# A fused attention, channel-mix and mixture-of-experts kernel: expert remainders of at most 32 rows move from full 128-row slots to small float32 slots on four quarters of TensorE's columns

## The chip, the cores and the metric

One core of one Trainium2 chip. The metric is the device time of one execution in microseconds (us), the median of several. A difference of about 0.2% is what a measurement of this kernel can tell from none.

## The reference, cut to what matters

Block-causal attention (4 batches, 8 heads, 576 tokens, head width 64) feeds a channel mix (512 to 1024 to 512, in float64 weights), and its output `x` feeds a mixture of 8 experts in which each token goes to one expert:

```python
fresh_e = argmax(logits[b, s]); e = fresh_e if s == 0 or local_gate[b, s] < 0.5 else prev_e
h = np.maximum(x[b, s] @ w1[e], 0.0)          # 512 -> 1024
out[b, s] = p[e] * (h @ w2[e])                # 1024 -> 512
```

There are 2304 tokens. On the inputs used, the reference sends 0, 1196, 0, 1, 361, 285, 457 and 4 tokens to experts 0 to 7.

## The kernel before

The kernel records its operations and a list scheduler (`schedule`, with estimated costs) puts them into one order per engine; each engine then runs its list strictly in order, held only by semaphores. Attention and channel mix come first, then the experts. All products are made to nearly float32 precision by splitting each operand into a high and a low float32r part (`split`: ACT copies the high part, DVE subtracts) and issuing three matmuls, high x high, high x low, low x high.

For the experts the tokens are sorted into *slots* of 128 rows of one expert. `dispatch` runs twice: early, after 7 of 9 token groups, for 7 slots that are certainly full, and late, for the rest. It computes on DVE, from counts and ranks, each token's slot and row, and by one matmul per token tile (`d_lh`, `d_rhs`) the lists `gidx` (rows to gather), `sidx` (rows to scatter) and `pslot` (weights), and the expert of each slot (`evi`). With the counts above the 22 slots of the main part (`MAIN`) hold experts 1 (6 slots), 4 (1), then 1 (4), 3 (1), 4 (2), 5 (3), 6 (4), 7 (1). Slots past `MAIN` stand in a branch that runs only when more are used.

`slot(j)` does one slot: POOL gathers 128 rows of `y_dram` (`xg`), SP loads the expert's `w1` and `w2` in eight pieces of 512 KB under the condition that the expert is not that of the slot before (`load`), ACT and DVE split the eight pieces, PE transposes the rows (4 instructions), multiplies by `w1` (24 matmuls of 128x512, accumulators `accB`), transposes the result twice 4, multiplies by `w2` (24 more), ACT scales, and POOL scatters. So a slot is 48 matmuls of 128x512 and 12 transposes, whether it holds 128 rows or one. Buffers of the attention phase are used again: `ring` names such as `xg`, `hs0`, `hs1`, `ot` cycle through `ea`, `wraw`, `relu`, `th` and `xm`. In the rows, `s` and `acc` are the accumulators, `psT` receives transposes, `attr`, `wvh`, `wkh`, `kkh`, `xh` and their partners hold split weights, `wrh`/`wrl` the split rows; `eb`, `qk`, `x`, `d` are the raw weight pieces.

Of the kernel before, what the change touches and what calls it, by code (L numbers as in the profile page):

```python
# [12 lines left out]
I32 = mybir.dt.int32  # L13
# [158 lines left out]
class Plan:  # L172
# [69 lines left out]
    @staticmethod  # L242
    def form(eng, op, outs, ins):


        if eng == "pe":
            full = op == "matmul" and ins[0].dtype == F32
            return 0.836 * outs[0].shape[0] + 3, -(-ins[0].shape[0] // 64), 2 if full else 1
        if eng == "pool":
            return op in ("tensor_tensor", "tensor_copy")  # L250
        if eng != "dve" or op in ("memset", "reduce_max", "reduce_sum", "tensor_reduce", "reciprocal",
                                  "tensor_tensor_scan"):
            return False
# [17 lines left out]
def fused_kernel(ctx: ExitStack, tc: tile.TileContext, a, out):  # L271
# [40 lines left out]
    def iota_f(where, name, shape, pattern, base, cm):  # L312
        ti = o_all.rearrange("p a b -> p (a b)").bitcast(I32)[:, 0:shape[1]]
        pool.iota(ti, pattern=pattern, base=base, channel_multiplier=cm)
        tf = where.tile(shape, F32, name=name)
        pool.tensor_copy(tf, ti)
        return tf
# [659 lines left out]
            after(9, lambda: dispatch(g < NG - 1))  # L977


    iota25 = iota_f(cst, "iota25", [128, SLOTS + 1], [[1, SLOTS + 1]], 0, 0)  # L980
# [4 lines left out]
    evi = [rt.tile([1, 2, n], I32, name=f"evi{i}") for i, n in enumerate(stages)]  # L985
# [9 lines left out]
    def dispatch(early):  # L995

        st = 0 if early else 1
        nt, j0, n = (EG * 2, 0, EARLY) if early else (NT, EARLY, SLOTS - EARLY)  # L1000
        mine = slice(j0, j0 + n)
# [15 lines left out]
        dve.tensor_copy(cf, ci)  # L1017
        end = small("end", [128, NE])
        dve.tensor_tensor_scan(end, cf, z8, 0.0, op0=ALU.add, op1=ALU.add)
        base = small("base", [128, NE])  # L1020
        dve.tensor_tensor(base, end, cf, op=ALU.subtract)
        if early:
            dve.tensor_scalar(end, end, float(EARLY), None, op0=ALU.min)
            dve.tensor_scalar(base, base, float(EARLY), None, op0=ALU.min)
            dve.tensor_tensor(taken, end, base, op=ALU.subtract)
            dve.tensor_scalar(taken, taken, 128.0, None, op0=ALU.mult)
            dve.tensor_scalar(base, base, 128.0, None, op0=ALU.mult)
        else:
            dve.tensor_scalar(base, base, 128.0, EARLY * 128.0, op0=ALU.mult, op1=ALU.add)
            dve.tensor_tensor(base, base, taken, op=ALU.subtract)  # L1030
            dve.tensor_scalar(used, end[0:1, NE - 1:NE], float(EARLY), None, op0=ALU.add)


        last = small("last", [1, 1])
        dve.tensor_scalar(last, end[0:1, NE - 1:NE], -1.0, None, op0=ALU.add)
        jj = small("jj", [1, SLOTS])[:, 0:n]
        dve.tensor_scalar(jj, iota25[0:1, 0:n], last, None, op0=ALU.min)
        ob = small("ob3", [128, SLOTS - 5, NE])
        cmp = ob[0:1, 0:n, :]
        dve.tensor_tensor(cmp, end[0:1, :].unsqueeze(1).to_broadcast([1, n, NE]),  # L1040
                          jj.unsqueeze(2).to_broadcast([1, n, NE]), op=ALU.is_le)
        dve.reduce_sum(es[:, j0 + 1:j0 + n + 1], cmp, axis=AX.X)
        dve.tensor_copy(evi[st][:, 0, :], es[:, j0 + 1:j0 + n + 1])
        dve.tensor_tensor(evi[st][:, 1, :], es[:, j0 + 1:j0 + n + 1], es[:, j0:j0 + n], op=ALU.not_equal)
# [11 lines left out]
        dve.scalar_tensor_tensor(posf, lim, 4096.0, posf, op0=ALU.mult, op1=ALU.add)  # L1056
        posi = small("posi", [128, 2, NT], I32)[:, :, 0:nt]
# [12 lines left out]
        dve.tensor_tensor(vals[:, ts, 2], p_all[:, ts], f(phr), op=ALU.subtract)  # L1070
        w = n + n % 2
        pinv = aux()
        for t in range(nt):
            lh = ring(rt, "d_lh", [128, 128], F32R, 2)
            dve.tensor_scalar(lh, iota128, pmd[:, 0, t:t + 1], None, op0=ALU.is_equal)
            sel = ring(rt, "d_sel", [128, 20], F32, 2)[:, 0:w]
            dve.tensor_scalar(sel, iota25[:, j0:j0 + w], pmd[:, 1, t:t + 1], None, op0=ALU.is_equal)
            rhs = ring(rt, "d_rhs", [128, 60], F32R, 3)[:, 0:3 * w].rearrange("p (k w) -> p k w", k=3)
# [3 lines left out]
        inv = small("inv", [128, 60])[:, 0:3 * w].rearrange("p (k w) -> p k w", k=3)  # L1082
# [3 lines left out]
        dve.tensor_tensor(pslot[st], inv[:, 1, 0:n], inv[:, 2, 0:n], op=ALU.add)  # L1086


    def units():
# [128 lines left out]
    def slot(j, always):  # L1218
# [94 lines left out]
```

## Time and profile before

| what | value |
|---|---|
| median of 3 runs | 817.48 us (816.93 to 818.48) |
| the profiled execution's own time | 818.0 us |
| its span, first to last instruction | 816.3 us |
| mean granted TensorE clock | 0.991 |
| PE busy | 795.9 us, 97% of the span |
| DVE busy | 640.1 us, 78% |

The profiled execution is 0.5 us above the median and spends 1.7 us outside its span. Sums are made against the span and then carried to the median. In rows of the timeline the first two numbers are the start and the time in us; a row with x2 or more merges neighbours of one form, from the first start to the last end. Matmul records overlap, so the price of one in a stream is the distance between two starts, not its own time. In rows of matmuls 128\*128 is rows x columns of the stationary operand.

### The profile page before, as it was taken

What the parts mean: (1) busy time and instruction counts of PE and PEld (TensorE: products, weight loads), DVE (VectorE), ACT (ScalarE), POOL (GpSimd) and SP (SyncE); (2) the same over time, 40 slices, a digit from 0 to 9 for tenths busy, and PEclk for the clock granted to TensorE, in tenths of its full rate; (3) what the DMA queues carried; (4) which work ended last, traced back from release to release, by engine and by line L of the source; (5) the groups of instructions that cost most, each with busy time, mean ns of one, the idle gap of its engine ahead of it and who ended that gap; (6) DMA issues with size and microseconds to landing.
All of it is one profiled execution on the core that took longest, in us unless ns stands there. A gap on an engine that the chain in (4) does not pass through costs nothing. (4 is left out here: it accounts for less than half of the span.)

```text
span 816.3 us, 14710 instructions
## 1 busy us (share of the span) xinstructions
PE 795.9 (97%) x4911; PEld 660.3 (81%) x4911; DVE 640.1 (78%) x1350; ACT 561.7 (69%) x1186; POOL 302.2 (37%) x271
## 2 busy tenths in 40 slices
PE   9999999999999999999999997999999999999996
PEld 8665798988889989788998886778777877878774
DVE  7987767775799767687776498799999889898860
ACT  3888567883679845366883425577888889889861
POOL 3443675542646526355433345021412222222010
PEclk9999999999999999999999998999999999999998
DMA  7574312210322212101300016101571676170520
GB/s 214 163 210 147 104 56 98 72 51 27 104 77 85 79 36 82 48 28 54 105 22 27 1 42 221 47 27 40 196 294 53 213 277 211 55 252 32 174 86 10
DMA packets 37167, 83.98 MB, mean 103 GB/s; under 512 B 6174, under 2 KB 10270, under 8 KB 37088
## 3 DMA queue, kind: packets, MB, share of 16 engines
q1 hardware_dynamic: 33568, 72.52, 27.3%
q0 software_dynamic: 3520, 10.49, 3.8%
q8 instruction: 40, 0.66, 0.3%
q14 instruction: 39, 0.32, 0.1%
HBM read 132.27 MB, written 10.49 MB: 175 GB/s over the span
## 5 line engine op out<-in xcount | busy, mean ns | idle before, releaser
L267 DVE TENSOR_REDUCE nm<-s 128x1 f32<-128x576 f32 (+4 forms) x132 | 67.6, 546 | 23.5 <-ACT s L267 22.3
L267 PE MATMUL acc<-xh,wkh 128*128 128x256 f32 x288 | 81.4, 293 | 1.9 <-DVE lg L267 1.0
L267 PE MATMUL acc<-xl,wkh 128*128 128x256 f32 x288 | 81.4, 291 | 0.1
L267 PE MATMUL acc<-xh,wkl 128*128 128x256 f32 x288 | 80.1, 287 | 0.0
L267 POOL TENSOR_TENSOR attr<-qk,attr 64x512 fp32r<-64x512 f32 (+1 forms) x48 | 65.6, 1367 | 37.7 <-ACT attr L267 30.3
L267 PE MATMUL av<-attr 128*128 128x256 f32 (+3 forms) x336 | 77.3, 288 | 0.8 <-ACT x L267 0.3
L267 DVE TENSOR_TENSOR attr<-psT,attr 64x256 fp32r<-64x256 f32 (+2 forms) x120 | 63.0, 526 | 17.1 <-ACT attr L267 14.3
L267 POOL TENSOR_TENSOR kkl<-relu,kkh 128x512 fp32r<-128x512 f32 x36 | 48.0, 1336 | 57.5 <-ACT kkh L267 49.1
L267 PE MATMUL s<-attr 128*128 128x288 f32 (+3 forms) x288 | 67.2, 301 | 0.6 <-ACT ea L267 0.6
L267 POOL TENSOR_TENSOR xl<-xm,xh 128x512 fp32r<-128x512 f32 x36 | 46.7, 1298 | 49.7 <-ACT xh L267 45.9
L267 PE MATMUL acc<-attr,wrh 128*128 128x512 f32 x176 | 61.5, 408 | 1.1 <-ACT wrh L267 1.1
L267 ACT ACTIVATE attr<-psT 64x256 fp32r<-64x256 f32 (+2 forms) x120 | 52.9, 462 | 10.4 <-PE psT L267 9.4
L267 ACT ACTIVATE xh<-xm 128x512 fp32r<-128x512 f32 x36 | 22.7, 630 | 53.1 <-DVE xm L267 53.0
L267 PE MATMUL acc<-wvh,kkh 128*128 128x512 f32 x144 | 56.6, 414 | 0.0
L267 PEld LDWEIGHTS acc<-xh,wkh 128*128 128x128 f32 x288 | 53.2, 189 | 4.1 <-DVE lg L267 1.2
L267 PEld LDWEIGHTS av<-attr 128*128 128x128 f32 (+1 forms) x336 | 51.5, 166 | 5.2 <-DVE x L267 0.7
L267 PE MATMUL acc<-wvl,kkh 128*128 128x512 f32 x144 | 55.6, 408 | 0.0
L267 PE MATMUL acc<-wvh,kkl 128*128 128x512 f32 x144 | 55.4, 408 | 0.0
L267 DVE TENSOR_TENSOR wrl<-psT,wrh 128x512 fp32r<-128x512 f32 x66 | 45.0, 683 | 13.2 <-ACT wrh L267 13.1
L267 PE MATMUL psT<-ident,eb 128*128 128x128 f32 (+1 forms) x288 | 54.4, 278 | 0.0
L267 PEld LDWEIGHTS acc<-xl,wkh 128*128 128x128 f32 x288 | 53.5, 189 | 1.1 <-POOL xl L267 0.4
L267 PEld LDWEIGHTS acc<-xh,wkl 128*128 128x128 f32 x288 | 53.5, 189 | 0.4
(308 smaller groups left out, 2499.9 us busy)
## 6 DMA issues: line engine op xcount, KB each, us to landing
x<-in_w SPq DMA_DIRECT2D x88, 512.0 KB
eb<-in_w SPq DMA_DIRECT2D x44, 512.0 KB
qk<-in_qk SPq DMA_DIRECT2D x24, 544.0 KB
qk<-in_w SPq DMA_DIRECT2D x22, 512.0 KB
d<-in_w SPq DMA_DIRECT2D x22, 512.0 KB
y_dram<-th SPq DMA_DIRECT2D x18, 256.0 KB
v<-in_v SPq DMA_DIRECT2D x28, 160.0 KB
relu<-in_w_mix SPq DMA_DIRECT2D x14, 256.0 KB
```

Source lines behind the costliest of these rows:

```text
L267: o[2](*o[3], **o[4])
```

## The change

- `MAIN` goes from 22 to 19, and the late `dispatch` finds experts whose remainder after full slots is at most `ROWS` = 32 rows; up to `SMALLS` = 3 of them go to small slots. With the counts above these are expert 3 (1 row), 5 (29 rows) and 7 (4 rows), and the 19 full slots are all used.
- A small slot gathers 32 rows, transposes them, and multiplies without splitting, in float32, with 32 stationary columns: quarter `t` of the output (partitions 32t to 32t+31) takes a quarter of the output columns. It loads its expert's weights always, in sixteen pieces of 256 KB through four buffers (`pieces`), so in four rounds of four; each round is followed by one group of matmuls (`tiles`): 8 of 32x256 in each round of `w1`, 16 of 32x128 in each round of `w2`.
- The small slots stand in the program before full slots 10, 13 and 15. `xg` falls from 3 buffers to 2, `hs0`, `hs1` and `ot` from 2 to 1, which frees the four buffers. The scheduler's assumed time of a full slot's weight piece falls from some 1500 ns to 400 ns; a small slot's is 800 ns.

The diff, cut to its core:

```diff
-MAIN = 22
+MAIN = 19
+SMALLS, ROWS = 3, 32
+BEFORE = (EARLY + 3, EARLY + 6, EARLY + 8)
...
+        if op == "tiles":
+            return 30.0, 3, 1
...
+        if not early:
+            dve.scalar_tensor_tensor(ci, pc[:, 0:NE], 127.0 - ROWS, taken, op0=ALU.add, op1=ALU.subtract)
+            dve.tensor_scalar(ci, ci, 7, None, op0=ALU.logical_shift_right)
...
+            dve.tensor_copy(rest, ci)
+            dve.tensor_tensor(rest, cf, rest, op=ALU.subtract)
+            dve.tensor_tensor_scan(upto, rest, z8, 0.0, op0=ALU.add, op1=ALU.add)
+            dve.scalar_tensor_tensor(rest, upto, float(SMALLS), rest, op0=ALU.is_le, op1=ALU.mult)
+            dve.tensor_tensor(cf, cf, rest, op=ALU.subtract)
+            dve.tensor_scalar(upto_s, upto, float(SMALLS), None, op0=ALU.min)
...
+        if not early:
+            dve.tensor_tensor(ob, o, limit.unsqueeze(1).to_broadcast([128, nt, NE]), op=ALU.mult)
+            dve.reduce_sum(lim, ob, axis=AX.X)
+            dve.tensor_tensor(lim, rank, lim, op=ALU.is_ge)
+            dve.tensor_tensor(ob, o, away.unsqueeze(1).to_broadcast([128, nt, NE]), op=ALU.mult)
...
-    rings["xg"] = [0, of("ea", 0), of("ea", 1), of("wraw", 0)]
-    rings["hs0"], rings["hs1"] = [0, of("relu", 0), of("th", 0)], [0, of("relu", 1), of("th", 1)]
-    rings["ot"] = [0, flat(of("xm", 0)), of("wraw", 1)]
+    rings["xg"] = [0, of("ea", 0), of("ea", 1)]
+    rings["hs0"], rings["hs1"] = [0, of("relu", 0)], [0, of("th", 0)]
+    rings["ot"] = [0, flat(of("xm", 0))]
+
+    pieces = [of("wraw", 0), of("wraw", 1), of("relu", 1), of("th", 1)]
...
-        plan.add("sp", "load", issue, outs=[raw], after=[at])
+        plan.add("sp", "load", issue, outs=[raw], after=[at], hold=800.0 if j >= SLOTS else 400.0)
...
+    def tiles(ns, count, out, ins, stationary, moving):
...
+        def issue():
+            for i in ns:
+                for t in range(4):
+                    nc.tensor.matmul(out[t * ROWS:t * ROWS + ROWS, :], stationary(i, t), moving(i, t),
+                                     start=(i == 0), stop=(i == count - 1))
+
+        plan.add("pe", "tiles", issue, outs=[out], ins=ins + [out] * (ns[0] > 0), hold=1000.0)
...
+        for i in range(2):
+            for n in range(4):
+                c, ns = 2 * i + n // 2, slice(n % 2 * 512, n % 2 * 512 + 512)
+                load(j, pieces[n], lambda e, c=c, ns=ns: a["w1"][bass.ds(e, 1), c * 128:(c + 1) * 128, ns]
+                     .rearrange("o p n -> p (o n)"), at)
+            tiles((2 * i, 2 * i + 1), 4, po, [small_x, *pieces], lambda c, t: small_x[:, c * ROWS:c * ROWS + ROWS],
+                  lambda c, t: pieces[c % 2 * 2 + t // 2][:, t % 2 * 256:t % 2 * 256 + 256])
+        act.activation(small_h, po, AF.Relu)
...
     for j in range(MAIN):
+        if j in BEFORE:
+            small_slot(BEFORE.index(j))
         slot(j, j == 0)
```

How the instructions stand after the change is taken from the two built programs; the numbers in names are buffer numbers. On PE, the second round of the first small slot, among the full slots' products (`s`, `acc` are the accumulators of two full slots in flight; `s_0_133` is the small slot's own):

```order
L273 MATMUL acc_150<-attr,wrh 128x512
L273 MATMUL s_0_145<-kkl_157,wrh 128x512
L273 MATMUL acc_150<-attr,wrl 128x512
L273 MATMUL s_0_145<-xl_154,wrh 128x512
L1319 MATMUL s_0_133<-wraw_129,v_132 32x256 x2
L1319 MATMUL s_0_133<-wraw_130,v_132 32x256 x2
L1319 MATMUL s_0_133<-relu_126,v_132 32x256 x2
L1319 MATMUL s_0_133<-th_124,v_132 32x256 x2
L273 MATMUL s_0_145<-kkl_157,wrl 128x512
L273 MATMUL s_0_145<-kkl_157,wrh 128x512
```

The four `L1319` rows are new: eight matmuls that take all four pieces, with 23 rows of full-slot work since the round before. Twelve such groups stand in the program, and PE's list holds 48 matmuls of 32x256 and 96 of 32x128 more, and 144 of 128x512 and 36 transposes of full slots fewer.

On SP's list, the loads around the second and third round of the second small slot (`wraw`, `relu_126`, `th_124` are its pieces, the rest are pieces of full slots 14 to 16):

```order
L1256 DMA qk_131<-in_w 128x1024
L1256 ISA
L1256 DMA wraw_129<-in_w 128x512
L1256 ISA
L1256 DMA wraw_130<-in_w 128x512
L1256 ISA
L1256 DMA relu_126<-in_w 128x512
L1256 ISA
L1256 DMA th_124<-in_w 128x512
L1256 ISA
L1256 DMA d_127<-in_w 128x2x512
```

Before, this list holds full slots' pieces alone; now each round's four loads wait there for the PE group that reads the pieces' last contents, and the full slots' loads stand behind them.

On DVE, the beginning of the late `dispatch` (`d_` names are its small tiles, `wkl`, `wvl`, `wrl` are splits for full slots). Before:

```order
L267 SCALAR_TENSOR_TENSOR d_ci_174<-av_139,taken 128x8
L267 TENSOR_TENSOR vals<-p_all,d_phr_185 128x4
L267 TENSOR_SCALAR d_ci_174<-d_ci_174 128x8
L267 CAST d_cf_175<-d_ci_174 128x8
L267 SCALAR_TENSOR_TENSOR d_end_176<-d_cf_175,z_105 128x8
L267 TENSOR_SCALAR d_last_178<-d_end_176 1x1
```

After:

```order
L273 CAST d_cf_176<-d_ci_175 128x8
L273 SCALAR_TENSOR_TENSOR d_ci_175<-av_140,taken 128x8
L273 TENSOR_SCALAR d_ci_175<-d_ci_175 128x8
L273 CAST ssum_0_143<-d_ci_175 128x8
L273 TENSOR_TENSOR wkl<-x_1_122,wkh 128x1024
L273 TENSOR_TENSOR ssum_0_143<-d_cf_176,ssum_0_143 128x8
L273 SCALAR_TENSOR_TENSOR ssum_0_143<-ssum_0_143,z_105 128x8
L273 TENSOR_TENSOR wvl<-eb_146,wvh 128x1024
L273 SCALAR_TENSOR_TENSOR ssum_0_143<-ssum_0_143 128x8
L273 TENSOR_SCALAR ssum_1_144<-ssum_0_143 128x8
L273 TENSOR_SCALAR ssum_0_148<-ssum_0_143 128x8
L273 TENSOR_TENSOR wrl<-psT_138,wrh 128x512
```

The count of slots (`d_end`) now comes after nine more small operations, with splits between them; in all the late dispatch holds 29 operations more on DVE: 4 over 128x144 elements, 3 over 128x18, one cast of 128x128, and 21 over 128x8 or less. Its 36 operations that make `d_sel` and `d_rhs` grow from 18 and 54 columns to 22 and 66.

## Rows read from the trace of the kernel before

**Rows 1.** The page, part 1: busy time of each engine.

```profile
span 816.3 us, 14710 instructions
PE 795.9 (97%) x4911; PEld 660.3 (81%) x4911; DVE 640.1 (78%) x1350; ACT 561.7 (69%) x1186; POOL 302.2 (37%) x271
```

**Rows 2.** Windows of the experts' stage: busy time by engine, clock, DMA share, GB/s.

```profile
core 0: us, PE busy (x) PEld busy (x) DVE busy (x) ACT busy (x) POOL busy (x), PEclk, DMA share, GB/s
500.00:520.00 20.00, 18.60 (x75) 14.73 (x75) 13.75 (x32) 9.57 (x13) 7.53 (x4) 0.83 0.18 55
540.00:560.00 20.00, 20.00 (x101) 15.72 (x101) 19.67 (x62) 15.68 (x21) 4.56 (x3) 1.00 0.09 28
560.00:580.00 20.00, 20.00 (x105) 16.17 (x105) 20.00 (x60) 16.97 (x22) 5.26 (x3) 1.00 0.16 54
580.00:600.00 20.00, 19.24 (x92) 15.04 (x90) 19.92 (x20) 15.01 (x21) 5.08 (x3) 1.00 0.93 332
592.00:604.00 12.00, 11.58 (x56) 8.76 (x55) 11.68 (x12) 9.83 (x14) 2.86 (x2) 1.00 1.02 393
640.00:760.00 120.00, 120.00 (x574) 95.44 (x573) 107.92 (x106) 102.53 (x133) 27.14 (x19) 1.00 0.52 177
```

**Rows 3.** Timeline of SP's queue: loads of a slot's first weight pieces.

```profile
487.35 0.97 SPq L1189 DMA_DIRECT2D eb<-in_w  x2
...
713.20 2.37 SPq L1189 DMA_DIRECT2D eb<-in_w  x2
...
725.71 2.09 SPq L1189 DMA_DIRECT2D eb<-in_w  x2
...
763.44 2.37 SPq L1189 DMA_DIRECT2D eb<-in_w  x2
```

**Rows 4.** Timeline of PE in a full slot: consecutive products.

```profile
746.73 0.39 PE L267 MATMUL acc<-wvl,wrh 128*128 128x512 f32 x1
746.95 0.39 PE L267 MATMUL s<-wkh,wrh 128*128 128x512 f32 x1
747.18 0.39 PE L267 MATMUL acc<-wvh,wrl 128*128 128x512 f32 x1
```

**Rows 5.** Timeline of PE: float32 matmuls with 64 and 128 stationary columns.

```profile
4.58 1.15 PE L267 MATMUL s<-qk 128*64 128x64 f32 x16 [0.81 <-DVE smask L267]
...
44.99 1.03 PE L267 MATMUL acc<-x,v 128*64 128x256 f32 x4
...
52.52 0.65 PE L267 MATMUL acc<-x 128*64 128x256 f32 x2
...
72.98 0.59 PE L267 MATMUL av<-d,v 128*64 128x256 f32 x2
...
525.25 1.06 PE L267 MATMUL av<-wg,relu 128*128 128x9 f32 x8
```

**Rows 6.** Groups of PE by form, 0 to 90 us: records, busy us, mean ns.

```profile
L267 PE MATMUL acc<-x,v 128*64 128x256 f32 x16 | 4.9, 395 | 0.0
...
L267 PE MATMUL s<-qk 128*64 128x64 f32 x32 | 2.4, 275 | 0.8 <-DVE smask L267 0.8
```

**Rows 7.** Timeline of DVE in the late dispatch.

```profile
542.06 0.17 DVE L267 TENSOR_SCALAR d_ci<-d_ci 128x8 int32<-128x8 int32 x1
542.26 0.17 DVE L267 CAST d_cf<-d_ci 128x8 f32<-128x8 int32 x1
...
546.31 0.16 DVE L267 TENSOR_TENSOR evi<-es 1x18 int32<-1x18 f32 x1
546.40 0.16 DVE L267 CAST evi<-es 1x18 int32<-1x18 f32 x1
...
548.42 0.29 DVE L267 TENSOR_TENSOR d_ob<-o_all,d_base 128x144 f32<-128x144 f32 x1
548.64 0.16 DVE L267 TENSOR_TENSOR d_lim<-rank_all,d_lim 128x18 f32<-128x18 f32 x1
```

**Rows 8.** Timeline of PE: matmuls with a wait before them, in brackets.

```profile
587.59 0.51 PE L267 MATMUL s<-wkh,wrl 128*128 128x512 f32 x1 [0.56 <-DVE wrl L267]
...
600.91 0.50 PE L267 MATMUL s<-kkh,wrl 128*128 128x512 f32 x1 [0.22 <-DVE wrl L267]
```

**Rows 9.** Timeline of ACT: the first split of the first slot.

```profile
491.05 1.06 ACT L267 ACTIVATE attr<-eb 128x1024 fp32r<-128x1024 f32 x1 [0.85 <-DMA eb<-in_w]
```

More of the change, by code (lines that the diff above doesn't have):

```diff
@@ L984, in fused_kernel, with of_small @@
     stages = (EARLY, SLOTS - EARLY)
-    evi = [rt.tile([1, 2, n], I32, name=f"evi{i}") for i, n in enumerate(stages)]
+    evi = [rt.tile([1, 2, n], I32, name=f"evi{i}") for i, n in enumerate((EARLY, SLOTS - EARLY + SMALLS))]
+    quarter = rt.tile([128, 1], F32, name="quarter")
+    for t in range(4):
+        pool.memset(quarter[32 * t:32 * t + 32, :], t - 4.0)
+    def of_small():
+        x = flat(buffers(a1, "ssum1", [128, 2, H], F32, 2)[2])
+        return x[:, 0:SMALLS].bitcast(I32), x[:, 4:4 + SMALLS].bitcast(I32), x[:, 8:8 + SMALLS]
     gidx = [rt.tile([128, n], I32, name=f"gidx{i}") for i, n in enumerate(stages)]
@@ L1000, in dispatch @@
         nt, j0, n = (EG * 2, 0, EARLY) if early else (NT, EARLY, SLOTS - EARLY)
+        m = n if early else n + SMALLS
+        gidx_s, sidx_s, pslot_s = of_small()
         mine = slice(j0, j0 + n)
@@ L1017, in dispatch @@
         dve.tensor_copy(cf, ci)
+        if not early:
+            dve.scalar_tensor_tensor(ci, pc[:, 0:NE], 127.0 - ROWS, taken, op0=ALU.add, op1=ALU.subtract)
+            dve.tensor_scalar(ci, ci, 7, None, op0=ALU.logical_shift_right)
+            (rest, upto), (upto_s, limit), (away, _) = ((x[:, 0, :], x[:, 1, :]) for n in ("ssum0", "ssum1")
+                                                        for x in rings[n][1:3] if x is not rings["ssum1"][2])
+            dve.tensor_copy(rest, ci)
[4 more added lines that the diff above has]
+            dve.tensor_scalar(upto_s, upto, float(SMALLS), None, op0=ALU.min)
         end = small("end", [128, NE])
@@ L1056, in dispatch @@
         dve.scalar_tensor_tensor(posf, lim, 4096.0, posf, op0=ALU.mult, op1=ALU.add)
+        if not early:
+            dve.tensor_tensor(ob, o, limit.unsqueeze(1).to_broadcast([128, nt, NE]), op=ALU.mult)
+            dve.reduce_sum(lim, ob, axis=AX.X)
+            dve.tensor_tensor(lim, rank, lim, op=ALU.is_ge)
+            dve.tensor_tensor(ob, o, away.unsqueeze(1).to_broadcast([128, nt, NE]), op=ALU.mult)
+            far = f(small("phr", [128, NT], F32R))
+            dve.reduce_sum(far, ob, axis=AX.X)
+            dve.tensor_tensor(far, far, lim, op=ALU.mult)
+            dve.tensor_tensor(posf, posf, far, op=ALU.add)
         posi = small("posi", [128, 2, NT], I32)[:, :, 0:nt]
@@ L1075, in dispatch @@
             dve.tensor_scalar(lh, iota128, pmd[:, 0, t:t + 1], None, op0=ALU.is_equal)
-            sel = ring(rt, "d_sel", [128, 20], F32, 2)[:, 0:w]
+            sel = ring(rt, "d_sel", [128, 22], F32, 2)[:, 0:w]
             dve.tensor_scalar(sel, iota25[:, j0:j0 + w], pmd[:, 1, t:t + 1], None, op0=ALU.is_equal)
-            rhs = ring(rt, "d_rhs", [128, 60], F32R, 3)[:, 0:3 * w].rearrange("p (k w) -> p k w", k=3)
+            rhs = ring(rt, "d_rhs", [128, 66], F32R, 3)[:, 0:3 * w].rearrange("p (k w) -> p k w", k=3)
             dve.tensor_tensor(rhs, sel.unsqueeze(1).to_broadcast([128, 3, w]),
@@ L1086, in dispatch @@
         dve.tensor_tensor(pslot[st], inv[:, 1, 0:n], inv[:, 2, 0:n], op=ALU.add)
+        if not early:
+            dve.tensor_scalar(gidx_s, inv[:, 0, n:m], -1.0, 0.0, op0=ALU.add, op1=ALU.max)
+            lh = ring(rt, "d_lh", [128, 128], F32R, 2)
+            dve.tensor_copy(lh.rearrange("p (t r) -> p t r", r=ROWS),
+                            ident[:, 0:ROWS].unsqueeze(1).to_broadcast([128, 4, ROWS]))
+            pr = aux()
+            pe.matmul(pr[:, 0:3 * SMALLS], f(lh), inv[:, :, n:m], start=True, stop=True)
+            dve.tensor_scalar(sidx_s, pr[:, 0:SMALLS], 4.0, quarter, op0=ALU.mult, op1=ALU.add)
+            dve.tensor_copy(inv[:, 0, 0:SMALLS], pr[:, SMALLS:2 * SMALLS])
+            dve.tensor_tensor(pslot_s, inv[:, 0, 0:SMALLS], pr[:, 2 * SMALLS:3 * SMALLS], op=ALU.add)
     def units():
@@ L1244, in slot, with small_slot @@
         scatter(j, ot)
+    def tiles(ns, count, out, ins, stationary, moving):
+        def issue():
+            for i in ns:
+                for t in range(4):
+                    nc.tensor.matmul(out[t * ROWS:t * ROWS + ROWS, :], stationary(i, t), moving(i, t),
+                                     start=(i == 0), stop=(i == count - 1))
+        plan.add("pe", "tiles", issue, outs=[out], ins=ins + [out] * (ns[0] > 0), hold=1000.0)
+    gidx_s, sidx_s, pslot_s = of_small()
+    def small_slot(q):
+        j = SLOTS + q
+        x = turn("xg")[0:ROWS, :]
+        rows = gidx_s[0:ROWS, q:q + 1]
+        plan.add("pool", "gather", lambda: nc.gpsimd.indirect_dma_start(
+            out=x, out_offset=None, in_=y_dram,
+            in_offset=bass.IndirectOffsetOnAxis(ap=rows.bitcast(U32), axis=0),
+            bounds_check=T - 1, oob_is_err=False),
+            outs=[x], ins=[rows, y_dram], hold=1200.0, late=3600.0)
+        at = expert(j, True)
+        ps = turn("ptB")
+        for c in range(4):
+            pe.transpose(ps[:, c * ROWS:c * ROWS + ROWS], x[:, c * 128:c * 128 + 128], ident[0:ROWS, 0:ROWS])
+        act.copy(small_x, ps[:, 0:4 * ROWS])
+        po = of("s1", 0)[:, 0:256]
+        for i in range(2):
[6 more added lines that the diff above has]
+        act.activation(small_h, po, AF.Relu)
+        ps = turn("ptB")
+        for i in range(2):
+            pe.transpose(ps[:, i * 128:i * 128 + 128], small_h[:, i * 128:i * 128 + 128], ident)
+        act.copy(small_t, ps[:, 0:256])
+        po = of("av", 0)[:, 0:128]
+        for i in range(2):
+            for n in range(4):
+                k = 4 * i + n
+                load(j, pieces[n], lambda e, k=k: a["w2"][bass.ds(e, 1), k * 128:(k + 1) * 128, :]
+                     .rearrange("o p n -> p (o n)"), at)
+            tiles(range(4 * i, 4 * i + 4), 8, po, [small_t, *pieces],
+                  lambda k, t: small_t[:, k % 2 * 128 + k // 2 * ROWS:k % 2 * 128 + k // 2 * ROWS + ROWS],
+                  lambda k, t: pieces[k % 4][:, t * 128:t * 128 + 128])
+        act.activation(small_o, po, AF.Copy, scale=pslot_s[:, q:q + 1])
+        to = sidx_s[:, q:q + 1]
+        quarters = out.rearrange("t (c n) -> (t c) n", c=4)
+        plan.add("pool", "scatter", lambda: nc.gpsimd.indirect_dma_start(
+            out=quarters, out_offset=bass.IndirectOffsetOnAxis(ap=to.bitcast(U32), axis=0),
+            in_=small_o, in_offset=None, bounds_check=4 * T - 1, oob_is_err=False),
+            outs=[quarters], ins=[to, small_o], hold=1200.0, late=3600.0)
```

39 lines of the change are left out of this document (25 added, 14 removed).

## The prediction

> **What bounds the kernel now.** I read the page first: PE is busy 97% of the span, the next engine 78% [rows 1]. Busy PE alone says little, so I went to the windows of the experts' stage. From 640 to 760 us PE has no idle time, while the DMA engines are half used, and DVE and ACT are at 90% and 85% [rows 2]. There PE sets the pace. Earlier it does not: from 540 to 600 us, while the late dispatch runs between the splits, DVE is at 98 to 100%, and in the last third of that PE begins to wait for it [rows 2, 8]. Last, SP's queue shows the beat of the slots: the first weight pieces of slots 17 to 21 are issued from 713.20 to 763.44 us, four slots in 50.24 us [rows 3]. A full slot costs 12.56 us of a PE that never waits, and products start 0.225 us apart [rows 4], so 48 of them make 10.8 us and the transposes most of the rest.
>
> **What goes.** Three full slots: 3 x 12.56 = 37.7 us of PE. They go from the stretch where PE sets the pace, so they count in full.
>
> **What comes on PE.** No row shows a matmul with 32 stationary columns, so I price it from both sides. The nearest are float32 matmuls with 64 columns. Each gives two records: the eight `s<-qk` matmuls of a batch make 16 [rows 5]. Four records of 128x256 take 1.03 us, and one lasts 0.395, so starts are (1.03 - 0.395) / 3 = 0.212 us apart [rows 5, 6]; for 128 moving columns I take half, 0.106. A small slot has 16 matmuls of 32x256 and 32 of 32x128, that is 32 and 64 records: 32 x 0.212 + 64 x 0.106 = 13.6 us if nothing overlaps. If the four quarters stream at once it is a quarter, 3.4 us. Loading the stationary columns is no tighter bound: eight records with 128 columns and only 9 moving ones take 1.06 us [rows 5], at most 0.13 each, so at most 0.033 for 32 columns, 96 x 0.033 = 3.2 us.
>
> Between these ends I choose by the order of the records. `tiles` issues quarter 0, 1, 2, 3, and a matmul's two records stand next to each other on one quarter. If records start in the order of the list, the second has to wait until its own quarter has finished the first, and the next quarter's first record can only run beside it. Then two stream at a time, and a round costs one record more than its matmuls: 2 x 9 x 0.212 + 2 x 17 x 0.106 = 7.4 us. The row that is nearest does not decide: `s<-qk` changes between two halves of the columns, and its 16 records are (1.15 - 0.275) / 15 = 0.058 us apart [rows 5, 6], which is both a quarter of 0.212 with no overlap and half of 0.13 for loading 64 columns.
>
> The Trainium skill, page "TensorE: Matmul & The Clock Gate", section "Part 3: Packing small matmuls — row/col tiling", says that matmuls on different column tiles run concurrently and gives 2.38 times for three tiles of 32 columns; no run here shows it yet. By that, some 3.2 times for four, as an estimate, the 13.6 us would be 4.3, near the fourfold case below.
>
> Around them come six transposes per small slot, at most 0.13 us each by the same row [rows 5], say 0.7 us, and eight changes between full and quarter arrays. Two records of 64 columns behind others of 64 take 0.59 us, behind 128 columns 0.65 [rows 5]: 0.06 us a change. A narrower tile may cost more; I take 0.1, so 0.8 us per small slot (0.5 to 1.2).
>
> The Trainium skill, page "TensorEngine Tiling (Array Packing)", section "Key Properties", says that a change of tiling mode drains the engine. The rows show 0.06 us; a full drain would be the 0.39 us of a product less its 0.225 us to the next start, 0.17 us, and the 24 changes would cost 4.0 us instead of 2.4.
>
> So a small slot costs 7.4 + 0.7 + 0.8 = 8.9 us with pairs, 4.9 with all four quarters, 15.1 with none. Three cost 26.7, 14.7 or 45.3 us. I take 26.7.
>
> **What comes on DVE.** The late dispatch has 29 operations more. The small ones start 0.09 us apart when they do not hang on each other, 0.20 us when they do; one over 128x144 takes 0.22 us to the next start [rows 7]. The order puts splits between most steps, which hides the dependence, so 21 x 0.12 + 4 x 0.22 + 3 x 0.09 + 0.2 for the cast, and some 0.3 for the wider `d_sel` and `d_rhs`: 4.2 us (3.6 to 5.9). What would hide it is idle time of DVE, and from 540 to 600 us it has 0.4 us of that [rows 2]. At 587.59 us PE waits 0.56 us for a split of DVE, again at 600.91 [rows 8], so PE has no lead left there, and what delays DVE delays PE. I take 4 us. It would be nothing if the full slots' products had lead that these rows do not show, and 6 at most.
>
> **What comes on SP and the DMA queue.** The full slots load 6 experts instead of 8, the small slots load 3 more: 9 x 4.2 MB against 8. A small slot's pieces have one set of buffers, so each round's loads wait for the PE group before. The first split of the first slot waited for its piece until 491.05 us, 3.7 us after the issue at 487.35 [rows 3, 9]. Of that the 0.52 MB take 1.3 us at 393 GB/s [rows 2], so some 2.4 us are fixed; a round of 1.05 MB needs 2.4 + 2.7 = 5.1 us. The order shows 23 rows of full-slot products between the first two groups, some 24 x 0.225 = 5.4 us: hidden, barely. Five of the nine gaps between rounds are that short. Slots 13 and 15 load 4.2 MB each in the same stretch, and a round queued behind 1 to 1.5 MB of that comes 2.7 to 4 us late. PE then stands, with the full slots' products behind the group. I take 2 us in all, with 0 and 15 (five rounds, 3 us each) as bounds. The single buffers of `ot`, `hs0` and `hs1` are written a slot later, 12.56 us, so I cost them at nothing; a scatter of that length would make ACT and then PE wait.
>
> **The clock.** From 500 to 520 us the granted clock is 0.83 on average [rows 2], one stretch at 1.2 instead of 2.4 GHz behind the waits of the early dispatch. The order of PE changes a little there; one such stretch more or less is 17% of 20 us at half speed, some 2 us either way. I take 0.
>
> **The sum.** -37.7 + 26.7 + 4 + 2 = -5.0 us: the span goes from 816.3 to 811.3. The profiled execution (818.0) is 0.5 above the median, and I carry the difference to the median: 817.48 - 5.0 = **812.5 us**.
>
> **The rivals.** *All four quarters stream at once* (-37.7 + 14.7 + 6 = -17.0): 800.5 us. For it: nothing in the rows forbids it; against it: the two records of a matmul share a quarter. *No overlap* (-37.7 + 45.3 + 6 = +13.6): 831.1 us, slower. For it: `s<-qk` shows no overlap between two halves; against it: the weight load explains that row as well. It decides from a small slot of (37.7 - 6) / 3 = 10.6 us on, that is 9.1 us of matmuls, an overlap of 1.5. *The rounds come late*: pairs as forecast, but loads at 14 us instead of 2: 824 us. For it: one set of buffers, full loads in the same queue; against it: the DMA engines are half idle. *The change does not do what it says*: 19 slots are used exactly; one token counted otherwise and the branch runs six more slots, 6 x 12.56, some 888 us. Against it: 22 of 22 held before.
>
> **How the numbers follow.** Pairs 0.40, all four 0.30, none 0.13, late rounds 0.10, branch 0.02, others 0.05. The range from 798 to 828 us takes in pairs, four quarters and late rounds with their bounds and leaves out the serial case and the branch, 0.15, and little else. Within 0.2% is 1.6 us. Faster: all of the fourfold case, 0.29 of the pairs, 0.03 of the rest, 0.62. Same: 0.07 of the pairs and 0.03, 0.10. Slower: 0.28.
>
> **What will show it.** The starts of the `L1319` records: 0.106 and 0.212 us apart within a matmul and nearly none between quarters means pairs; a group lasts 1.9 us with pairs, 0.85 with four, 3.4 with none. The beat of full slots with no small one between stays at 12.56 us. DVE's late dispatch ends some 4 us or more later, and PE waits for DVE between 570 and 610 us. PE's waits for `wraw`, `relu` or `th` pieces sum to about 2 us. I am wrong if quarters behave in neither way, if a switch costs far more than 0.1 us, or if PE shows no wait for DVE there.

## The result, and the profile after

The changed kernel takes 808.70 us (median of 4 runs, 807.52 to 810.18), the kernel before 817.43 us beside it: a ratio of 0.9893, 95% interval 0.9872 to 0.9913, or 8.7 us less. On another chip (e11 below) the ratio was 0.9883, 0.9868 to 0.9898. The profiled execution took 808.18 us, its span fell from 816.3 to 806.4, by 9.9 us.

The page of the changed kernel, first part, and its windows over stretches that were shown of before:

```profile
span 806.4 us, 15002 instructions
PE 778.0 (96%) x5040; PEld 640.3 (79%) x5040; DVE 609.6 (76%) x1346; ACT 535.3 (66%) x1156; POOL 299.9 (37%) x275
...
core 0: us, PE busy (x) PEld busy (x) DVE busy (x) ACT busy (x) POOL busy (x), PEclk, DMA share, GB/s
500.00:520.00 20.00, 16.74 (x63) 13.65 (x64) 13.52 (x32) 7.58 (x11) 7.03 (x4) 0.74 0.13 42
580.00:600.00 20.00, 19.53 (x101) 15.90 (x101) 20.00 (x60) 11.79 (x16) 2.66 (x2) 1.00 0.58 198
592.00:604.00 12.00, 9.62 (x47) 7.30 (x45) 11.17 (x18) 5.33 (x8) 2.89 (x2) 1.00 0.78 279
640.00:760.00 120.00, 118.47 (x753) 87.66 (x752) 90.81 (x90) 91.08 (x123) 26.25 (x21) 1.00 0.72 239
```

Against [rows 1, 2] PE is busy 17.9 us less in all, but from 500 to 520 and from 592 to 604 us it is idle 1.9 and 2.0 us more, and from 640 to 760 us, where it had no idle time, 1.5 us. The DMA engines carry 239 instead of 177 GB/s there. To see where the 9.9 us lie I cut both spans at the same products: the first `w2` product of slot 0, of slot 9 (the last one with no group ahead of it) and of the last slot. Of before:

```profile
533.39 0.40 PE L267 MATMUL s<-wkh,wrh 128*128 128x512 f32 x1
...
650.57 0.40 PE L267 MATMUL s<-kkh,wrh 128*128 128x512 f32 x1
...
801.79 0.40 PE L267 MATMUL s<-kkh,wrh 128*128 128x512 f32 x1
```

and after:

```profile
534.88 0.50 PE L273 MATMUL s<-wkh,wrh 128*128 128x512 f32 x1
...
654.03 0.40 PE L273 MATMUL s<-kkh,wrh 128*128 128x512 f32 x1
...
788.70 0.39 PE L273 MATMUL s<-wkh,wrh 128*128 128x512 f32 x1
```

- Up to slot 0: 1.5 us more.
- From slot 0 to slot 9: 119.1 instead of 117.2 us, 1.9 more.
- From slot 9 to the last: 134.7 instead of 151.2 us. Three full slots are 37.7 us, so the three small ones cost 134.7 - (151.2 - 37.7) = 21.2 us, 7.1 each.
- From there to the end: 17.7 instead of 14.5 us, 3.2 more.

Sum: 1.5 + 1.9 + 21.2 + 3.2 - 37.7 = -9.9 us, the whole difference. A second trace of the changed kernel (e11, span 809.7 us) gives 3.5, 2.8, 21.6 and 3.1 us for the same four terms: the small slots and the end repeat, the first two terms vary by 1 to 2 us from execution to execution.

**The groups.** The timeline of PE in the changed kernel, at two `w1` rounds of the first small slot and one `w2` round:

```profile
656.67 0.63 PE L273 MATMUL psT<-ident,ea 128*128 128x128 f32 x4
657.23 0.64 PE L1319 MATMUL s<-wraw,v 128*32 128x256 f32 x8
657.69 0.39 PE L1319 MATMUL s<-relu,v 128*32 128x256 f32 x2
657.70 0.39 PE L1319 MATMUL s<-th,v 128*32 128x256 f32 x2
657.90 0.39 PE L1319 MATMUL s<-relu,v 128*32 128x256 f32 x2
657.92 0.39 PE L1319 MATMUL s<-th,v 128*32 128x256 f32 x2
658.23 0.49 PE L273 MATMUL s<-xh,wrh 128*128 128x512 f32 x1
...
663.76 0.40 PE L273 MATMUL s<-xl,wrh 128*128 128x512 f32 x1
664.88 1.27 PE L1319 MATMUL s<-wraw,v 128*32 128x256 f32 x8 [0.72 <-DMA wraw<-in_w]
666.16 0.63 PE L1319 MATMUL s<-relu,v 128*32 128x256 f32 x4
666.80 0.63 PE L1319 MATMUL s<-th,v 128*32 128x256 f32 x4
667.36 0.50 PE L273 MATMUL s<-kkl,wrl 128*128 128x512 f32 x1
...
672.74 0.40 PE L273 MATMUL acc<-attr,wrl 128*128 128x512 f32 x1
673.06 0.65 PE L1319 MATMUL av<-wraw,x 128*32 128x128 f32 x16
673.52 0.40 PE L1319 MATMUL av<-relu,x 128*32 128x128 f32 x8
673.74 0.40 PE L1319 MATMUL av<-th,x 128*32 128x128 f32 x8
674.07 0.66 PE L273 MATMUL psT<-ident,ea 128*128 128x128 f32 x4
```

At 657.23 the sixteen records of a round begin within 0.69 us: in the trace four start within 0.02 us, one on each quarter, the next four 0.22 us later. All four quarters stream at once. From the instruction before the group to the one after it is 1.20 to 1.35 us, in nine of the twelve groups. The group at 664.88 takes 3.6 us: its pieces land one after another, each quarter runs as its piece comes, and the overlap is gone with the wait. The trace has a second one of 3.5 us at 709.09 and one of 1.65 at 735.52. The twelve sum to 20.5 us; with 1.26 and 1.335 us on time for the two kinds they would be 15.6.

### The profile page after: what moved, and what is told of

It is laid out like the page before. It is cut to its first block, busy times and chain, and to the rows that moved or that the text cites. A ratio compares the mean times of both kernels' runs of the same rounds, so it can differ in the third digit from the quotient of the medians.

```text
span 806.4 us, 15002 instructions
## 1 busy us (share of the span) xinstructions
PE 778.0 (96%) x5040; PEld 640.3 (79%) x5040; DVE 609.6 (76%) x1346; ACT 535.3 (66%) x1156; POOL 299.9 (37%) x275
## 4 chain that ended last, share of the span: by engine, by line
PE 67%; issue 11%; DVE 11%; DMA 6%; ACT 2%; POOL 1%; SPq 1%; POOLq 0%; ACTq 0%; DVEq 0%
PE acc L273 38%; PE s L273 12%; PE psT L273 9%; PE av L273 6%; DMA out<-xm,sidx 2%; PE acc L1379 1%; DVE wvl L273 1%; DVE attr L273 1%; DVE xm L273 1%; DMA out<-v,ssum 1%; DVE wrl L273 1%; DMA wraw<-in_w 1%; DMA x<-in_w 1%; ACT attr L273 1%; DVE relu L273 1%
## 5 line engine op out<-in xcount | busy, mean ns | idle before, releaser
L1236 POOL DMA_INDIRECT out<-xm,sidx x19 | 26.3, 1383 | 147.6 <-ACT xm L273 124.9
L273 PE MATMUL acc<-attr,wrh 128*128 128x512 f32 x160 | 56.7, 405 | 1.1 <-ACT wrh L273 1.1
```

Of the source, the lines that this page charges most:

```text
L273: o[2](*o[3], **o[4])
L1236: plan.add("pool", "scatter", lambda: nc.gpsimd.indirect_dma_start(out=out, out_offset=bass.IndirectOffsetOnAxis(ap=at.bitcast(U32), axis= ...
```

## The experiments

Each time is the median; the ratio goes against the kernel before on the same chip. Two edits recur: the time that the scheduler assumes for a load, which moves instructions and nothing else, and the branch.

**e1: no small slots.**

```diff
-        if j in BEFORE:
-            small_slot(BEFORE.index(j))
```

> Leaves out: the three small slots, so the 34 rows of the remainders of experts 3, 5 and 7 are not written. All else of the change stays (19 full slots, the longer late dispatch, the single buffers, the assumed load times). Theory A (from the trace after the change: between slots 9 and 18 a small slot costs 7.2 us): the time falls from 808.7 by 3 x 7.2 = 21.7 to 787.0 us, and what remains against before is -37.7 for the full slots, +3.4 up to slot 9, +3.1 at the end = 786.2. Theory B (my forecast: 8.9 us each and 2 us of load waits): it falls by 28.7 to 780.0 us. Theory C (all four quarters and nothing else, 4.9 us each): by 14.7 to 794.0 us.

Measured 790.89 us, ratio 0.9660 (0.9641 to 0.9679), so the small slots cost 0.0233 x 817.4 = 19.0 us by the ratios. That is between theories A and C, nearest to A, and excludes B. Its profile says more: slot 9 to 18 takes 113.7 us, 20.9 less than after the change, 7.0 for a small slot. But slot 0 starts 4.2 us later than in the changed kernel, at a granted clock of 0.91 from 320 to 360 us and 0.71 from 500 to 520, and slot 0 to 9 takes 122.6 instead of 119.1 us, at a granted clock of 0.91 instead of 1.00 from 600 to 620 us. Both lie ahead of the small slots, and the total carries them too: it shows less than the small slots cost. The profiled execution was the slowest of the five, some 3 us above the median.

**e2: three slots in the branch.**

```diff
-        for j in range(MAIN, SLOTS):
+        for j in range(MAIN, MAIN + 3):
```

> Leaves out slots 22 to 24 of the branch, which does not run with these inputs; the main part's lists stay as they are. Theory A (at the end of the changed kernel GpSimd has to wait at the join of the branch for all eight of its transfer semaphores, the last scatter's among them, before it begins its closing work of 4.7 us; with three slots in the branch it waits for six): the time falls by 3.1 to 805.6 us, and the stretch from the last slot's start to the end goes from 17.7 back to 14.6 us. Theory B (the last scatter's landing bounds the end anyway, or the longer end has another cause): 808.7 us, no change.

Measured 806.13 us, ratio 0.9850 (0.9831 to 0.9869), 3.5 us below the changed kernel; last slot to end: 14.5 us. Theory A holds. GpSimd's records at the end (start, duration, instruction), of the changed kernel and of e2; `DMA_INDIRECT` is the last scatter, which raises the semaphore named when it has landed, and `EVENT_SEMAPHORE` waits for those behind it:

```
changed kernel
796.88 0.98 DMA_INDIRECT semaphore=115
797.47 3.12 EVENT_SEMAPHORE $S[117]>= $S[115]>=
800.81 1.06 INC_SWDGE_SEM
801.90 3.65 DRAIN
e2
798.08 0.98 DMA_INDIRECT semaphore=115
798.67 0.04 EVENT_SEMAPHORE $S[118]>= $S[116]>=
798.84 1.07 INC_SWDGE_SEM
799.94 3.65 DRAIN
```

The branch isn't taken, but its join waits for all the transfer semaphores that the branch's list uses. With 12 transfers in it those are all eight, the last scatter's among them, and the closing 4.7 us begin only after its landing. With 6 transfers that semaphore isn't among them, as before, and the closing work runs beside the landing.

**e3: the late dispatch's new operations alone, in the kernel before.**

```diff
-MAIN = 19
+MAIN = 22
-            dve.scalar_tensor_tensor(ci, pc[:, 0:NE], 127.0 - ROWS, taken, op0=ALU.add, op1=ALU.subtract)
+            dve.scalar_tensor_tensor(ci, pc[:, 0:NE], 127.0, taken, op0=ALU.add, op1=ALU.subtract)
...
-        if j in BEFORE:
-            small_slot(BEFORE.index(j))
```

with `rings` and the assumed load times of before.

> The kernel before with the late dispatch's new operations alone: 22 full slots, limit for small remainders 0 rows, no small slot, buffers and assumed load times as before. Theory A (the trace after the change: the stretch from slot 0 to slot 9 is 1.9 us longer, because the pieces of slots 6 and 7 are freed later by VectorE): 817.4 + 1.9 = 819.3 us. Theory B (my forecast of the term): + 4 to 821.4 us. Theory C (the longer stretch comes from the other parts of the change, the small slot's loads or the changed order): 817.4 us, no change.

Measured 820.51 us, ratio 1.0033 (1.0020 to 1.0047): 2.7 us more, 1.6 to 3.8. Theory A (1.9) lies within, my 4 us just above, and theory C (no change) is excluded. In its trace the cost stands where theory A has it: slot 0 to slot 9 takes 119.3 us, 2.1 more than before, and slot 9 to 18 takes 113.1 us in both.

**e4: the assumed load time of before.**

```diff
-        plan.add("sp", "load", issue, outs=[raw], after=[at], hold=800.0 if j >= SLOTS else 400.0)
+        plan.add("sp", "load", issue, outs=[raw], after=[at], hold=800.0 if j >= SLOTS else None)
```

> The changed kernel with the scheduler's assumed time of a full slot's piece as before (some 1500 instead of 400 ns); nothing left out. Theory A (the assumed 400 ns lets splits of slot 0 stand ahead of the early dispatch's last operations on VectorE, and TensorE waits 2.1 us longer there): slot 0 starts 1.5 us earlier, 807.2 us. Theory B (the shorter assumption also makes the late dispatch's stretch later): up to 3.4 us, 805.3 us. Theory C (the assumption was shortened for the stretch with small slots, whose loads come later without it): slower, 810 us or more.

Measured 823.19 us, ratio 1.0064 (1.0046 to 1.0082): 14 us slower than the changed kernel. Theory A is right for slot 0 (532.5 instead of 534.9 us), and theory C for the rest: slot 9 to 18 takes 150.8 us, 12.4 for a small slot instead of 7.1. The waits of its PE from 654 to 801 us (total, times, longest):

```profile
PE psT L273 <- ACT th L273: 3.6, 3, 1.6
PE s L1319 <- DMA wraw<-in_w: 3.1, 2, 2.2
PE s L273 <- ACT wrh L273: 2.6, 3, 1.3
PE psT L273 <- ACT x L273: 2.3, 5, 0.6
```

The two `w1` rounds of the second small slot stand back to back in that order, and this one group of 32 records took 8.0 us from the instruction before it to the one after. Part of the price is the clock: from 640 to 760 us the granted clock is 0.94 here, and 1.00 before and after the change:

```profile
640.00:760.00 120.00, 108.69 (x654) 79.32 (x652) 83.43 (x81) 83.46 (x113) 22.46 (x19) 0.94 0.63 214
```

PE had waited 2.19 us for a piece until 717.41 us, and from 720 to 740 us the granted clock is 0.76. A mean of 0.94 over 120 us is some 7 us of work at full speed less, an estimate, and an upper bound, since PE also waits there. So the line that looks like bookkeeping decides the sign: without it the change is slower than before.

**e5: all on one quarter.**

```diff
-                    nc.tensor.matmul(out[t * ROWS:t * ROWS + ROWS, :], stationary(i, t), moving(i, t),
-                                     start=(i == 0), stop=(i == count - 1))
+                    nc.tensor.matmul(out[0:ROWS, :], stationary(i, t), moving(i, t),
+                                     start=True, stop=True)
```

> The changed kernel with all matmuls of the small slots on the first quarter of the columns, each overwriting the one before; the output rows of the small slots are not those of the reference. The order of all instructions is that of the changed kernel. Theory A (after the change the four quarters stream at once, groups of 0.9 us; a record takes 0.212 us for 256 columns and 0.106 for 128 when nothing overlaps): each of the 12 groups takes 3.4 instead of 0.9 us, + 30 us, less some 3 us that the late rounds wait already, so some 836 us; the records of a group are 0.212 or 0.106 us apart. Theory B (something else than the quarters made the groups short, such as a cost of a 32-column record far below that of 64 columns): no change, 809 us.

Measured 836.69 us, ratio 1.0213 (1.0187 to 1.0239). Theory A forecast 836. A `w2` group in its timeline:

```profile
681.16 1.93 PE L1319 MATMUL av<-wraw,x 128*32 128x128 f32 x16
682.93 1.04 PE L1319 MATMUL av<-relu,x 128*32 128x128 f32 x8
683.80 1.04 PE L1319 MATMUL av<-th,x 128*32 128x128 f32 x8
684.77 0.66 PE L273 MATMUL psT<-ident,ea 128*128 128x128 f32 x4
```

The 32 records stand 0.11 us apart and take 3.6 us to the next instruction, against 1.0 in the row at 673.06 above. So a record of 32 stationary columns is no cheaper than one of 64 ([rows 5, 6]: 0.106 estimated), and the quarters are worth 26 us.

**e6: quarter by quarter.**

```diff
-            for i in ns:
-                for t in range(4):
+            for t in range(4):
+                for i in ns:
```

> The changed kernel with the two loops of a group exchanged: all matmuls of quarter 0 first, then those of quarter 1, 2, 3; nothing left out. Theory A (a quarter's record waits for its own quarter alone and those of the others pass it): no change, 809 us, the first record of quarter 1 starts beside the first of quarter 0. Theory B (records start in the order of the list, and one that has to wait for its quarter holds all that stand behind it): a group of 16 records takes 13 x 0.212 = 2.8 us instead of 0.9, one of 32 records 29 x 0.106 = 3.1 us, in all + 24 us, some 833 us. That is also what my forecast of pairs supposed of the order within a matmul.

Measured 820.37 us, ratio 1.0023 (1.0007 to 1.0039), 10.6 us slower than the changed kernel, and neither theory. Its timeline, the first `w1` round and the beginning of a `w2` round:

```profile
658.41 0.66 PE L1319 MATMUL s<-wraw,v 128*32 128x256 f32 x8
658.87 0.39 PE L1319 MATMUL s<-relu,v 128*32 128x256 f32 x2
658.89 0.39 PE L1319 MATMUL s<-th,v 128*32 128x256 f32 x2
...
673.82 0.62 PE L1319 MATMUL av<-wraw,x 128*32 128x128 f32 x4
674.28 0.27 PE L1319 MATMUL av<-relu,x 128*32 128x128 f32 x1
674.28 0.30 PE L1319 MATMUL av<-wraw,x 128*32 128x128 f32 x1
674.39 0.27 PE L1319 MATMUL av<-relu,x 128*32 128x128 f32 x1
674.42 0.27 PE L1319 MATMUL av<-wraw,x 128*32 128x128 f32 x1
```

With four records to a quarter (the `w1` round) nothing is lost: 0.71 us from first to last start. With eight to a quarter, quarter 0 runs four alone, and at 674.28 quarter 1 starts beside its fifth; so on, two at a time: 8 + 3 x 4 = 20 steps of 0.11 us, 2.2 us in all. The records fit a small store at each quarter: four of its records stand there, and the fifth waits in the list with all behind it. That the pattern is so is shown; the store itself is inferred. The six `w2` groups take 2.71 instead of 1.335 us, 8.3 us in all; the six `w1` groups take 2.1 us more, nearly all of it in one late group at 712.48 us.

**e7: no loads after a small slot's first round.**

```diff
-                load(j, pieces[n], lambda e, c=c, ns=ns: a["w1"][bass.ds(e, 1), c * 128:(c + 1) * 128, ns]
+                if i == 0: load(j, pieces[n], lambda e, c=c, ns=ns: a["w1"][bass.ds(e, 1), c * 128:(c + 1) * 128, ns]
...
-                load(j, pieces[n], lambda e, k=k: a["w2"][bass.ds(e, 1), k * 128:(k + 1) * 128, :]
+                if False: load(j, pieces[n], lambda e, k=k: a["w2"][bass.ds(e, 1), k * 128:(k + 1) * 128, :]
```

> The changed kernel without the small slots' loads after their first round: the second round of w1 and both rounds of w2 multiply by the pieces of the first, so the output rows of the small slots are not those of the reference. Theory A (the two second rounds whose pieces came late cost 2.4 and 2.2 us, a third 0.3): 809 - 5 = 804 us, and all w1 groups take 1.2 to 1.3 us from the product before to the product after. Theory B (the late rounds only take the place of waits that the full slots would have elsewhere): 809 us. Theory C (the small slots' loads also hold up those of the full slots): below 803 us.

Measured 807.43 us, ratio 0.9863 (0.9833 to 0.9892), 2.5 us below the changed kernel with intervals that overlap. The second rounds of the first small slot ran in 1.33 us, but the second slot's first round now came late itself, with the next standing right behind it (32 records, 4.8 us). The groups summed to 17.5 us, 3.0 less. Inconclusive between A and B; theory C's time lies below the interval, which ends at 803.7 us.

**e8: two branches of three, and the old assumption for the early slots.**

```diff
-    with tc.If(count > MAIN):
+    for first in (MAIN, MAIN + 3):
+        with tc.If(count > first):
...
-        plan.add("sp", "load", issue, outs=[raw], after=[at], hold=800.0 if j >= SLOTS else 400.0)
+        plan.add("sp", "load", issue, outs=[raw], after=[at], hold=800.0 if j >= SLOTS else None if j < EARLY else 400.0)
```

> The changed kernel with two alterations, nothing left out: the six slots of the branch stand in two branches of three, and the assumed time of a piece is as before (some 1500 ns) for the seven slots of the early dispatch and 400 ns for the rest. Theory A (at the end GpSimd waits for six instead of eight semaphores, and slot 0 starts 2.4 us earlier as with the old assumption everywhere, while the small slots keep their places): 809.4 - 3.1 - 2.4 = 803.9 us. Theory B (a second branch costs as much as it saves): 807 us. Theory C (what the early dispatch gives back is lost in the late dispatch's stretch): 806.3 us.

Measured 805.52 us, ratio 0.9827 (0.9802 to 0.9853), 5.4 us below the changed kernel by the ratios. That is theory A's sum, but the trace shows smaller terms: slot 0 starts at 533.2 us, 1.7 earlier instead of 2.4, and the end is 1.7 us shorter instead of 3.1, because the second branch costs GpSimd 1.5 us (branch to branch, 796.34 to 797.86), half of what it saves. Slot 0 to 9 takes 0.6 us more, at a granted clock of 0.91 instead of 1.00 from 600 to 620 us. The span is 803.8 instead of 806.4 us, 2.5 less; where the rest of the 5.4 us comes from isn't shown.

**e9, e10, e11: more rows between the rounds, and the changed kernel beside them.** The edit of e9 against e8; e10 has 600.0 in place of the last 400.0.

```diff
-        plan.add("sp", "load", issue, outs=[raw], after=[at], hold=800.0 if j >= SLOTS else None if j < EARLY else 400.0)
+        plan.add("sp", "load", issue, outs=[raw], after=[at], hold=1200.0 if j >= SLOTS else None if j < EARLY else 400.0)
```

> The kernel of e8 with the assumed time of a small slot's piece 1200 instead of 800 ns, which puts 34 to 35 rows of TensorE's list between the two w1 rounds of the first two small slots where 29 and 30 stood; nothing left out. Theory A (a round's pieces take some 6 us to land, so about 6 rows more, 1.4 us, cover most of the two late rounds of 2.2 and 2.7 us): 2 to 4 us less than e8, 0.978 to 0.980 of before. Theory B (the pieces are held up by the full slots' loads in the same queue, and the wait moves along with the place): as e8, 0.983 of before. Theory C (a longer assumption brings the full slots' splits late, as in e4): slower, 0.986 or more.

> The kernel of e9 with the assumed time of a full slot's piece in the late part 600 instead of 400 ns, which puts 36 to 40 rows between the rounds of the first small slot and 38 between two rounds of the second; nothing left out. Theory A: a little below e9, by 0 to 1 us, all groups at 1.2 to 1.35 us. Theory C (the splits of the full slots come late, as with the old assumption, which cost 13.8 us): slower than e8 by some us.

> The changed kernel itself beside e9 and e10 on the same chip, nothing left out: 0.987 to 0.991 of before if its ratio holds from chip to chip; its two late w1 rounds (3.6 and 3.5 us from product to product) come again if they hang on the order, and not if they were chance.

Measured: e9 810.68 us, 0.9911 (0.9883 to 0.9939); e10 807.29 us, 0.9873 (0.9858 to 0.9887); e11 809.40 us, 0.9883 (0.9868 to 0.9898), with its late groups at 668.01 and 712.72 us again (3.8 and 3.9 us). In e10 every group takes 1.2 to 1.4 us, 15.8 in sum: no late round is left. Yet slot 9 to 18 takes 136.9 us, more than in e8 (134.9). Of these 2 us the clock can explain nearly all: from 740 to 760 us its granted clock is 0.91 (1.00 in e8), some 1.8 us of work less as an estimate. The waits of e10's PE from 655 to 790 us, in place of those for the pieces:

```profile
PE psT L273 <- ACT x L273: 1.7, 2, 1.1
PE psT L273 <- ACT th L273: 1.4, 2, 0.7
PE s L273 <- ACT wrh L273: 0.7, 1, 0.7
```

So theory C, in e9 (where slot 9 to 18 takes 139.1 us, 0.91 from 740 to 760 us, too) more than in e10: the late rounds hang on the order, as e11 shows, and more rows do cover them, but in these orders PE waits for ACT's work on the full slots instead, 3.8 us in e10 and 5.0 in e9, and the clock falls. Why ACT is late there, by the loads or by its own list, stays open.

**e12: the old assumption for slots 0 to 9.** The edit against e8.

```diff
-        plan.add("sp", "load", issue, outs=[raw], after=[at], hold=800.0 if j >= SLOTS else None if j < EARLY else 400.0)
+        plan.add("sp", "load", issue, outs=[raw], after=[at], hold=800.0 if j >= SLOTS else None if j < 10 else 400.0)
```

> The kernel of e8 with the old assumed time (some 1500 ns) for slots 0 to 9 instead of 0 to 6, 400 ns from slot 10 on; nothing left out. The small slots' groups keep their distances in TensorE's list. Theory A (in the late dispatch's stretch the order made with the old assumption is better: slot 0 to slot 9 took 117.8 us in e4, 119.7 in e8): 1.9 us less than e8, 0.980 to 0.981 of before. Theory B (the difference between e4 and e8 there was chance, or the small slots' first loads take it back): as e8, 0.983.

Measured 803.83 us, ratio 0.9808 (0.9785 to 0.9830): the fastest here, 7.0 us below the changed kernel by the ratios. Against e8 the intervals overlap, and its profile does not show theory A: slot 0 to 9 takes 121.4 us there, more than in e8. The profiled execution was the slowest of the five, 3.6 us above the median. From 600 to 620 us, where PE waits 2.8 us for ACT, its granted clock is 0.83; in e8 it is 0.91 with a wait of 2.0 us. Without what that takes, 3.4 and 1.8 us as an estimate, the stretch is 118 us in both, as in e4 (117.8, granted clock 1.00 there). So the traces show no gain of the order itself over e8; whether e12 is faster at all stays open.

## Why the prediction was right, and where its terms were not

The direction and the bound were right: PE stays the pace, and full slots cost what I took for them (nine of them take 113.7 us in e1, 12.6 each). I said 812.5 us, it was 808.7; I said 5.0 us off the span, it was 9.9. The mechanism on PE was not the forecast one but that of the fourfold rival. Term by term:

- **Matmuls of a small slot: 7.4 us forecast, 3.7 measured.** The failed step is "If records start in the order of the list, the second has to wait until its own quarter has finished the first, and the next quarter's first record can only run beside it". A waiting second record does not hold the next quarter's first; e6 shows this up to four records a quarter. That was my fourfold rival with its 0.85 us a group; the timeline has 0.91. The Trainium skill, page "TensorE: Matmul & The Clock Gate", section "Part 3: Packing small matmuls — row/col tiling", says that matmuls on different tiles run concurrently, and here the trace agrees, with 26 us in e5. The same section says that matmuls start strictly in list order; e6's rows at 674.28 and 674.39 differ, where a record of quarter 1 starts before records of quarter 0 that stand ahead of it.
- **Switches and transposes: 1.5 us forecast, about 1 us by the trace.** A group on time takes 1.20 to 1.335 us between its neighbours; less 0.225 for a product and 0.91 for its stream, 0.07 to 0.2 us is left for two changes of the array, where I took 0.2. The four transposes of 32 rows start 0.06 to 0.09 us apart (654.58 to 654.79 us), below my 0.13. With 4.3 us of groups net of a product each, and still my 0.7 for transposes, a small slot on time is 5.0 us, the rival's 4.9. Three make 15.0 instead of the 26.7 of the sum: -11.7.
- **Late rounds: 2 us forecast, 21.2 - 15.0 = 6.2 measured**, +4.2. Of these 4.9 us are the late groups; the rest isn't located. I had named the mechanism ("hidden, barely") and the gap of 23 rows; the loads were issued 0.8 us after the group before had begun its last records, and the pieces of the round at 664.88 us took 6.1 us from issue to landing by the chain of waits, where I had 5.1. What I did not see is that covering them costs as much elsewhere in the orders that were tried (e9, e10).
- **VectorE: 4 us forecast, 1.9 in the profile, 2.7 in e3**, -2.1. The end of the late dispatch moved further than I said, and cost less:

```profile
592.42 0.17 DVE L273 TENSOR_SCALAR sidx<-d_inv 128x18 int32<-128x18 f32 x1
...
596.16 1.06 ACT L273 ACTIVATE wkh<-x 128x1024 fp32r<-128x1024 f32 x1 [2.51 <-DMA x<-in_w]
...
601.55 1.06 ACT L273 ACTIVATE wkh<-x 128x1024 fp32r<-128x1024 f32 x1 [2.50 <-DMA x<-in_w]
602.51 1.04 ACT L273 ACTIVATE wvh<-eb 128x1024 fp32r<-128x1024 f32 x1
603.46 0.67 ACT L273 ACTIVATE xm<-s,pslot 128x512 f32<-128x512 f32 x1
...
604.18 0.50 PE L273 MATMUL s<-kkh,wrh 128*128 128x512 f32 x1 [2.09 <-ACT xm L273]
```

The lists come at 592.42 us, 18 us later than the 574.23 of before, but the splits placed ahead of them keep PE fed. From 520 to 655 us PE has no wait for VectorE left, which was one of my own signs of being wrong: its waits there are for ACT, 2.1, 1.3 and 0.5 us. VectorE acts one step earlier, through the loads. `xm` is the single `ot` buffer, and at first I took the 2.09 us for its price. The rows say otherwise: ACT wrote `xm` right behind two splits, the first of which had waited 2.50 us for a weight piece; the scatter before it, at 587.31 us, was long done. In that stretch the DMA engines carry 198 GB/s instead of 332 ([rows 2], 580 to 600 us), so the pieces were asked for late. SP's queue shows what held them: from 575 to 605 us the loads wait 16.8 us for VectorE's splits, which free their buffers, in 13 waits of up to 3.6 us; before it was 17.4 us in 22 waits of at most 1.7. No row shows a cost of the single buffers, and e3, which has the buffers of before, takes as long from slot 0 to slot 9 (119.3 us against 119.1).
- **Not foreseen: 1.5 us up to slot 0 and 3.2 at the end.** The first is the shorter assumed load time, which puts a split of slot 0 ahead of the early dispatch's last operations: the longest of PE's waits for `d_rhs` there grew from 1.41 to 2.43 us. All traces bear this out: with the old assumption for the early slots (before, e3, e4, e8, e9, e10, e12) slot 0 starts between 532.3 and 534.2 us, with the shorter one (after, e1, e2, e5, e6, e7, e11) between 534.5 and 539.4, so 1.5 us is near the least that it cost. The second is the branch's join (e2). Both are by-products of lines that I had read as free.
- **The clock: 0 forecast, and 0 from 500 to 540 us.** The granted clock is 0.83 and 0.91 in the two halves before, 0.74 and 1.00 after, the same sum. My price for it was low: a mean of 0.83 over 20 us is 3.4 us of work less, not 2.

Sum of the misses: -11.7 + 4.2 - 2.1 + 1.5 + 3.2 = -4.9, from -5.0 to -9.9. The forecast was near by luck: the largest miss, small slots too dear by 11.7 us, stood against three terms that were too cheap.

## What to carry to other kernels

Small remainders on four column quarters pay here only if the quarters run at once (e5 is slower than before) and the list alternates them (so is e6): keep at most four records to a quarter in a row. They also need the order that the shorter assumption makes (e4). A number that only the scheduler reads can be worth more than the change it comes with, so test it by itself. Look at the granted clock of each stretch before a difference is put down to an order: in e4, e8 and e12 it fell at or behind a wait of PE of 2.0 to 2.8 us, so such a wait can cost more than its own length; with the 2.1 us before 604.18 us in the changed kernel it stayed at 1.00. Where transfers wait in a branch that never runs, count them: they can put a landing ahead of the program's closing work.

## What was not expected of the hardware

- Records on the four quarters started within 0.02 us of one another, and the order of the list held them back only from the fifth record of a quarter on (e6).
- A skipped branch with 12 transfers cost 3.2 us at the end, one with 6 no more than before; a second skipped branch cost 1.5 us (e2, e8).
- The granted clock differed ahead of all that was changed: 1.00, 0.96 and 0.91 from 320 to 360 us before, after and in e1. It is no property of the kernel: the second trace of the changed kernel (e11) has 1.00 there. I took no cause from it.
